# First batch of a Linformer attention and gated feed-forward kernel: fewer filler matmuls, head groups ordered by load landing, fewer visits in the second half

## The chip, the cores and the metric

The kernel runs on one core of a Trainium2 chip. The metric is the device time of one execution in microseconds. The profile's span (first to last instruction) is some 1.8 us shorter than the timed execution of the same run. In the profile's lines, PE is TensorE, DVE is VectorE, ACT is ScalarE and POOL is GpSimd, which issues most loads here. Each line gives start and length in us; brackets give the engine's idle time before it and what ended that wait.

## The reference, cut to what matters

```python
# q, k, v: (8 batches, 8 heads, 1024, 64); E, F: (64, 1024)
k_proj = np.einsum('ks,bhsd->bhkd', E, k)
v_proj = np.einsum('ks,bhsd->bhkd', F, v)
scores = scale * np.matmul(q, k_proj.transpose(0, 1, 3, 2))
attn = np.exp(scores - max); attn = attn / (sum + 1e-09)
x = np.matmul(attn, v_proj)      # then (8192, 512)
out = (sigmoid(x @ w_gate) * (x @ w_val)) @ w_out   # 512 -> 1536 -> 512
```

The attention of a batch is small; the feed-forward part (2304 matmuls of 512 columns) is what TensorE does for most of the time. In batches 1 to 7 the attention of the next batch is slipped between the feed-forward steps of the present one. Batch 0 has nothing to hide behind, so its first half (its "opening") is done before any feed-forward step can start.

## The kernel before

Parts that the change and the argument touch. A filler is a matmul whose result nobody reads:

```python
def busy(n):
    for _ in range(n):
        mm(FB[3], bank[FB[3]][:, 0:P], ident[:, :], ident[:, :], ["ident"])
```

The opening works on two groups R of four heads. `project` multiplies K or V by E or F, `qt` transposes Q, `sc` makes scores and exponentials, `den` their sums and reciprocals (VectorE: a reciprocal, a cast of it to bf16 and a step called the split, at L599, L605 and L610), `bc` spreads the reciprocals over partitions (ScalarE copies them out), `xo` multiplies by V and scales (VectorE):

```python
busy(20)
qt, sc, den, bc, xo = half_unit(0, whole)
for R in range(2):
    bk = whole.next()
    project(0, 0, [bk, bk], 0, R)
    busy(4)
    keep_k(bk, 0, R)
    turn_k(whole, R)
    busy(10 if R == 0 else 4)
...
qt(0, ("DVE", "ACT")); busy(6); sc(0)
qt(1, ("DVE", "DVE")); busy(6); sc(1)
den(0); busy(10); den(1); bc(0)
v_part(0)()            # V's first half: copies by ACT, DVE, ACT, DVE
busy(6); bc(1); xo(0); busy(4)
keep = v_part(1); keep()
```

The list of feed-forward steps of batch 0 starts with a pair of steps (four PSUM banks) and takes attention work at numbered slots: batch 0's second half at slots 5 to 10, batch 1's attention from 13 on:

```python
put(5, lambda: (qt2(0, ("DVE", "ACT")), qt2(1, ("DVE", "ACT"))))
put(6, lambda: sc2(0))
put(7, lambda: (den2(0), sc2(1)))
put(8, lambda: (den2(1), bc2(0)))
put(9, lambda: (xo2(0), bc2(1)))
put(10, lambda: xo2(1))
spots = (13, 14, 16, 16, 17, 18, 18, 21, 23, 24, 25)
# k_alone, turn_k, v_alone, sc(0), sc(1), den, split, bc(0), bc(1), xo(0), xo(1)
```

The softmax here doesn't subtract the row's maximum and nothing guards it: scores larger than these inputs give would overflow.

## Time and profile before

| | before |
|---|---|
| timed, median of 4 | 575.24 us (573.6 to 575.25) |
| span of the profiled run | 573.4 us |
| TensorE busy | 552.7 us, 96% |
| step after the first pair starts | 29.04 us |
| K of batch 1 is projected from | 57.05 us |
| V of batch 1 is projected from | 63.78 us |
| first output projection starts | 80.74 us |

The last four rows are starts of TensorE instructions in the timeline, counted from the span's start. They cut the head of the kernel in stages: the **opening** up to 29.04, the **second half** of batch 0 from there to 57.05 (28.01 us), and **batch 1's steps** from 63.78 to 80.74 (16.96 us). The lines that the prediction shows below are from this kernel.

### The profile page before, as it was taken

Reading aid. Unit: us, or ns where it says so; the run is one execution under the profiler, and the core shown is the slowest. Engines: PE = TensorE matmul, PEld = TensorE weight load, DVE = VectorE, ACT = ScalarE, POOL = GpSimd, SP = SyncE. Lnnn points to the kernel's source line nnn. Section 1 sums busy time; section 2 is a strip of 40 time slices with the busy share of each in tenths; the row PEclk is TensorE's granted clock in tenths of the full one; section 3 lists DMA queues with packets and bytes.
Section 4 is the critical chain, followed back from the end, with each engine's and each line's share of the span. In section 5 each row is a group of like instructions: output and inputs, shape, how many; then the busy total and the mean of one; then the engine's idle time right before and its main releaser. Section 6 shows DMA issues by size and latency. Waiting matters only on the chain.

```text
span 573.4 us, 7674 instructions
## 1 busy us (share of the span) xinstructions
PE 552.7 (96%) x2987; PEld 247.8 (43%) x3042; DVE 252.0 (44%) x403; ACT 176.5 (31%) x310; POOL 107.2 (19%) x148
## 2 busy tenths in 40 slices
PE   5799989999999999999999999999999999999997
PEld 5443434444444444444444444444444444444443
DVE  3546256325633546335452264434463354633332
ACT  2444641342224322333223422144223332222220
POOL 9400200104400071001800045000610007000000
PEclk9999999999999999999999999999999999999999
DMA  9999995964656169430696036660501101010012
GB/s 167 198 201 199 139 213 133 160 125 107 115 113 102 37 113 155 83 84 22 125 168 118 20 87 107 139 104 37 113 18 47 38 20 39 37 38 22 34 37 93
DMA packets 76421, 56.02 MB, mean 98 GB/s; under 512 B 34688, under 2 KB 67968, under 8 KB 76384
## 3 DMA queue, kind: packets, MB, share of 16 engines
q0 software_dynamic: 33984, 29.89, 34.5%
q1 hardware_dynamic: 42400, 25.63, 17.3%
q8 instruction: 24, 0.39, 0.3%
q14 instruction: 13, 0.11, 0.1%
HBM read 60.29 MB, written 16.78 MB: 134 GB/s over the span
## 4 chain that ended last, share of the span: by engine, by line
PE 95%; DVE 2%; issue 1%; DMA 1%; ACT 0%; SPq 0%; DVEq 0%
PE pF L227 87%; PE pA L227 7%; DMA EF<-in_F_dram 1%; DVE rden L786 1%; DVE xT L655 0%; DVE hT L941 0%; DVE rden L599 0%; ACT vpD L231 0%; DVE rhi L605 0%; DVE vpD L502 0%; DVE rhl L610 0%; DVE ost L968 0%; ACT qT L231 0%; SPq L314 0%; DVE rhi L795 0%
## 5 line engine op out<-in xcount | busy, mean ns | idle before, releaser
L941 DVE SCALAR_TENSOR_TENSOR hT<-sig,pF 128x512 bf16<-128x512 f32 x192 | 130.7, 685 | 202.3 <-PE pF L227 153.9
L231 ACT ACTIVATE sig<-pF 128x512 f32<-128x512 f32 x192 | 114.3, 599 | 318.3 <-PE pF L227 315.9
L227 PE MATMUL pF<-xT,wV 128*128 128x512 bf16 x751 | 195.9, 379 | 3.3 <-DVE hT L941 1.6
L227 PE MATMUL pF<-xT,wG 128*128 128x512 bf16 x748 | 194.8, 380 | 3.4 <-DVE xT L655 1.8
L227 PE MATMUL pF<-wO,hT 128*128 128x512 bf16 x750 | 173.9, 379 | 1.5 <-issue 0.8
L227 PEld LDWEIGHTS pF<-xT,wV 128*128 128x128 bf16 x768 | 75.1, 98 | 92.2 <-DVE hT L941 2.0
L227 PEld LDWEIGHTS pF<-wO,hT 128*128 128x128 bf16 x768 | 74.0, 98 | 93.0 <-issue 6.0
L227 PEld LDWEIGHTS pF<-xT,wG 128*128 128x128 bf16 x768 | 72.1, 98 | 97.2 <-issue 13.9
L832 POOL PARTITION_BROADCAST rb<-rrow x96 | 70.7, 798 | 217.1 <-DMA rrow<-rden 212.0
L968 DVE TENSOR_SCALAR ost<-pF 128x512 f32<-128x512 f32 x64 | 44.3, 692 | 103.0 <-PE pF L227 103.0
L857 DVE TENSOR_TENSOR xT<-pA,rb 128x512 bf16<-128x512 f32 x56 | 34.7, 681 | 0.0
L231 ACT ACTIVATE eT<-pA 128x512 bf16<-128x512 f32 x61 | 31.7, 602 | 8.9 <-PE pA L227 8.7
L786 DVE RECIPROCAL rden<-pA 128x128 f32<-128x128 f32 x28 | 23.7, 910 | 0.0
L245 POOL DMA_DIRECT2D KV<-in_v_dram x9 | 7.8, 875 | 84.9 <-PE pF L227 84.9
L227 PE MATMUL pA<-KV,EFT 128*64 128x512 bf16 (+2 forms) x168 | 16.0, 333 | 0.0
L245 POOL DMA_DIRECT2D KV<-in_k_dram x9 | 8.0, 890 | 36.8 <-PE pF L227 36.8
L231 ACT ACTIVATE kpd<-pA 64x1024 bf16<-64x1024 f32 x6 | 6.1, 1017 | 28.3 <-PE pA L227 28.3
L227 PE MATMUL pA<-qT,kpD 64*64 64x512 bf16 (+1 forms) x132 | 10.6, 373 | 1.2 <-ACT vpD L231 1.2
L227 PEld LDWEIGHTS pA<-KV,EFT 128*64 128x64 bf16 x168 | 8.3, 115 | 7.5 <-issue 3.6
L227 PE MATMUL pA<-eT,vpD 64*64 64x512 bf16 (+1 forms) x144 | 10.4, 364 | 0.2 <-DVE vpD L502 0.2
L231 ACT ACTIVATE vpD<-pA 64x512 bf16<-64x512 f32 (+2 forms) x20 | 9.7, 485 | 2.1 <-PE pA L227 1.7
L231 ACT ACTIVATE rb<-pA 128x512 f32<-128x512 f32 x14 | 7.4, 599 | 8.1 <-PE pA L227 8.1
(61 smaller groups left out, 97.5 us busy)
## 6 DMA issues: line engine op xcount, KB each, us to landing
out_dram<-ost SPq DMA_DIRECT2D x64, 256.0 KB, 2.1
Qb<-in_q_dram POOLq DMA_DIRECT2D x7, 1024.0 KB, 15.2
KV<-in_k_dram POOLq DMA_DIRECT2D x7, 1024.0 KB, 10.8
KV<-in_v_dram POOLq DMA_DIRECT2D x7, 1024.0 KB, 10.4
wO<-in_moe_w_out_dram POOLq DMA_DIRECT2D x1, 1536.0 KB, 12.2
wG<-in_moe_w_gate_dram POOLq DMA_DIRECT2D x5, 256.0 KB, 18.4
wV<-in_moe_w_val_dram POOLq DMA_DIRECT2D x5, 256.0 KB, 19.0
KV<-in_k_dram POOLq DMA_DIRECT2D x2, 512.0 KB, 7.8
```

The costliest lines, as they stand in the source:

```text
L227: return add("PE", lambda e: e.matmul(o, lhsT, rhs, **kw), r=r, x=[("bank", b)])
L231: return add("ACT", lambda e: e.activation(o, i, func, scale=scale), r=r, w=w, x=x)
L245: add("POOL", lambda e: e.dma_start(o, i), r=r, w=w, dma=sem)
L786: lambda e, cc=cc: e.reciprocal(rden[:, cc], bank[bk][:, cc]),
L832: lambda e, n=n, i=2 * rnd + c, j=j, parts=parts: e.partition_broadcast(rb[0:parts, n, :], rrow[32 * j : 32 * j + 1, i, :], channels=parts),
L857: lambda e, r=r, g=g, n=n, bk=bks[g]: e.tensor_tensor(xT[s][:, r, :, 256 * g : 256 * g + 256], bank[bk][:, :].rearrange("p (f c) -> p f c" ...
L941: lambda e: e.scalar_tensor_tensor(hT[blk % 2][:, m, :], sg[:, :], 1.0, bank[pv][:, :], ALU.add, ALU.mult,),
L968: lambda e: e.tensor_scalar(o[:, :], bank[pb][:, :], 0.5, None, op0=ALU.mult),
```

## The change

Its intent: take out matmuls that only keep the array busy, do each group's steps in the order in which the loads land, take V's first copies off VectorE (which carries the reciprocals), and serve the second half in fewer, larger visits that start one step sooner.

```diff
-        busy(20)
+        busy(6)
...
-            busy(4)
+            busy(3)
...
-            busy(10 if R == 0 else 4)
+            if R == 0:
+                busy(6)
...
         qt(0, ("DVE", "ACT"))
-        busy(6)
+        busy(3)
         sc(0)
         qt(1, ("DVE", "DVE"))
         busy(6)
+        den(0)
         sc(1)
-        den(0)
-        busy(10)
+        busy(4)
+        v_part(0, ["ACT"] * 4)
         den(1)
         bc(0)
-        v_part(0)()
-        busy(6)
-        bc(1)
+        busy(4)
         xo(0)
         busy(4)
-        keep = v_part(1)
-        keep()
+        bc(1)
+        busy(6)
+        v_part(1, ["ACT", "DVE", "ACT", "DVE"])
...
-                if blk == 0:
+                if blk <= 1:
                     ms = [[0, 1]] + ms[2:]
...
-                put(5, lambda: (qt2(0, ("DVE", "ACT")), qt2(1, ("DVE", "ACT"))))
-                put(6, lambda: sc2(0))
-                put(7, lambda: (den2(0), sc2(1)))
-                put(8, lambda: (den2(1), bc2(0)))
-                put(9, lambda: (xo2(0), bc2(1)))
-                put(10, lambda: xo2(1))
-                spots = (13, 14, 16, 16, 17, 18, 18, 21, 23, 24, 25)
+                put(4, lambda: (qt2(0, ("DVE", "ACT")), qt2(1, ("DVE", "ACT"))))
+                put(5, lambda: (sc2(0), sc2(1)))
+                put(6, den2)
+                put(8, lambda: (bc2(0), bc2(1)))
+                put(9, lambda: (xo2(0), xo2(1)))
+                spots = (12, 13, 15, 16, 17, 18, 18, 21, 22, 23, 24)
```

Cut: the new order of the PSUM banks in the opening, `den` for both groups at once, the order of the matmuls inside the first pair (all of a pair's first two input tiles, then the other two), and the slots of batch 2's loads and Q transposes, which move with the others. Since block 1 now starts with a pair too, its list has one slot less, and slot numbers from 12 on mean one step later than before. Old slot 16, used twice, stood for both V's projection and the first scores of batch 1; now they are at 15 and 16.

More of the change, by code (lines that the diff above doesn't have):

```diff
@@ L202, in bass_linformer_attn__then__ffn_glu_sigmoid_kernel @@
         whole = Ring(
-            (A0, A1)
-            + (A2, A3, F0, F1)
-            + (A0, A1)
-            + (F2, A2)
-            + (A3, A3)
-            + (F0, F1)
-            + (A0, A1)
-            + (A2, A0)
-            + (A3, F0)
-            + (F1, F2)
-            + (A1, A2)
-            + (A3, A0)
-            + (A1, A2)
+            (A0, A1, A2, A3, F0, F1)
+            + (A0, A1, F2, A2)
+            + (A3, F0, F1)
+            + (A0, A1, A3, F0)
+            + (A2, F2, A0, A1, F1)
+            + (A2, A3, A0, A1, A2, A3)
         )
@@ L582, in sc, with den @@
                     )
-            def den(R):
-                bk, pp = ring.next(), slice(64 * R, 64 * R + 64)
-                for n in (2 * R, 2 * R + 1):
+            def den(R=None):
+                bk = ring.next()
+                pp = slice(0, P) if R is None else slice(64 * R, 64 * R + 64)
+                for n in [2 * x + g for x in both(R) for g in range(2)]:
                     for c in range(4):
@@ L597, in den @@
                         )
-                dve(
-                    lambda e: e.reciprocal(rden[pp, 0:P], bank[bk][pp, 0:P]),
-                    [],
-                    [("rden", 0, R)],
-                    b=bk,
-                )
-                dve(
-                    lambda e: e.tensor_copy(rhi[pp, 0:P], rden[pp, 0:P]),
-                    [("rden", 0, R)],
-                    [("rhi", R)],
-                )
+                rd, ri, rl = ([k + (x,) for x in both(R)] for k in (("rden", 0), ("rhi",), ("rhl",)))
+                dve(lambda e: e.reciprocal(rden[pp, 0:P], bank[bk][pp, 0:P]), [], rd, b=bk)
+                dve(lambda e: e.tensor_copy(rhi[pp, 0:P], rden[pp, 0:P]), rd, ri)
                 dve(
                     lambda e: e.scalar_tensor_tensor(
-                        rhl[pp, 0:P], rhi[pp, 0:P], rows[pp, 3, 0:1], rden[pp, 0:P],
-                        ALU.mult, ALU.add,
-                    ),
-                    [("rden", 0, R), ("rhi", R), "rows"],
-                    [("rhl", R)],
+                        rhl[pp, 0:P],
+                        rhi[pp, 0:P],
+                        rows[pp, 3, 0:1],
+                        rden[pp, 0:P],
+                        ALU.mult,
+                        ALU.add,
+                    ),
+                    rd + ri + ["rows"],
+                    rl,
                 )
@@ L906, in mstep, with first_pair @@
             gate(blk, m, pbs["G"], pbs["V"])
-        def first_pair(between):
+        def first_pair(blk, between):
             pbs = {(m, n): ffn.next() for m in range(2) for n in "GV"}
-            for m in range(2):
-                for i in range(2):
+            for i in (0, 1), (2, 3):
+                for m in range(2):
                     for n in "GV":
-                        mm_one(0, m, i, n, pbs[m, n])
-                if m == 0:
-                    between()
-            for m in range(2):
-                for n in "GV":
-                    for i in (2, 3):
-                        mm_one(0, m, i, n, pbs[m, n])
-                gate(0, m, pbs[m, "G"], pbs[m, "V"])
+                        for ii in i:
+                            mm_one(blk, m, ii, n, pbs[m, n])
+                        if between:
+                            between()
+                            between = None
+                    if i == (2, 3):
+                        gate(blk, m, pbs[m, "G"], pbs[m, "V"])
         def mm_one(blk, m, i, n, pb):
@@ L989, in bass_linformer_attn__then__ffn_glu_sigmoid_kernel, with v_part @@
             project(0, 0, [bk, bk], 0, R)
-            busy(4)
+            busy(3)
             keep_k(bk, 0, R)
             turn_k(whole, R)
-            busy(10 if R == 0 else 4)
-        def v_part(R):
+            if R == 0:
+                busy(6)
+        def v_part(R, engines):
             bks = [whole.next(), whole.next()]
             project(1, 1, bks, 0, R)
-            return lambda: keep_v(bks, 0, ["ACT", "DVE", "ACT", "DVE"], R)
+            keep_v(bks, 0, engines, R)
         qt(0, ("DVE", "ACT"))
-        busy(6)
+        busy(3)
         sc(0)
@@ L1047, in bass_linformer_attn__then__ffn_glu_sigmoid_kernel @@
                     if len(m) == 2:
-                        todo.append(lambda: first_pair(lambda: xo(1)))
+                        todo.append(
+                            lambda blk=blk: first_pair(blk, None if blk else lambda: xo(1))
+                        )
                     else:
@@ L1078, in bass_linformer_attn__then__ffn_glu_sigmoid_kernel @@
             if b == 0:
-                put(17, lambda: load_next(2))
-                put(25, lambda: transpose_q(2))
+                put(16, lambda: load_next(2))
+                put(24, lambda: transpose_q(2))
             else:
```

## The prediction

> **What bounds the kernel now.** I read the page's first two parts first, then busy time by stage, then the chain of waits from start to end, and last the timeline of the stretches where that chain leaves TensorE. The page:
>
> ```profile
> PE 552.7 (96%) x2987; PEld 247.8 (43%) x3042; DVE 252.0 (44%) x403; ACT 176.5 (31%) x310; POOL 107.2 (19%) x148
> ...
> PE   5799989999999999999999999999999999999997
> ```
>
> TensorE is busy 96% of 573.4 us, and only the first slices (14.3 us each) show room. Busy time in four stretches: the opening up to the point where the first pair of feed-forward steps runs on without a stop, the rest of batch 0's attention, batch 1's attention beside it, and all the rest:
>
> ```profile
> 0.00:27.31 27.31, 17.92 (x241) 13.02 (x243) 13.94 (x49) 9.69 (x20) 19.75 (x33) 1.00 1.19 182
> 27.31:55.24 27.93, 26.60 (x181) 12.08 (x186) 14.95 (x25) 13.39 (x24) 0.00 (x0) 1.00 1.31 196
> 55.24:82.00 26.76, 23.84 (x151) 10.38 (x154) 11.49 (x17) 14.34 (x28) 3.65 (x4) 1.00 1.07 174
> 82.00:570.00 488.00, 484.36 (x2416) 212.32 (x2461) 210.90 (x312) 139.07 (x238) 83.82 (x111) 1.00 0.41 83
> ```
>
> The second column is the length, the third TensorE's busy time. TensorE idles 9.4, 1.3 and 2.9 us in the first three, and 3.6 us in the 488 us that the change does not touch. So the change can win some microseconds at the head, and nothing near 2% (11.5 us). Pieces of the chain of waits in the opening (start, length, what):
>
> ```profile
> 1.38 4.28 DMA EF<-in_F_dram
> 5.74 1.95 PE pA L227 x8
> 7.69 2.13 PE pF L227 x20
> ...
> 18.06 0.96 DVE rden L599
> 19.05 0.64 DVE rhi L605
> 19.71 0.34 DVE rhl L610
> 20.09 0.97 DVE rden L599
> ...
> 21.93 0.30 DVE vpD L502
> 22.37 0.41 PE pA L227 x8
> ...
> 26.49 0.69 DVE xT L655
> ```
>
> Twenty matmuls that compute nothing sit on the chain at 7.69; then two rounds of reciprocal, cast and split on VectorE follow one another, and V's copies come behind them. Later the chain leaves TensorE here (timeline; idle before it in brackets):
>
> ```profile
> 52.20 0.60 PE L227 MATMUL pF<-xT,wG 128*128 128x512 bf16 x2 [1.17 <-DVE xT L655]
> 66.55 0.41 PE L227 MATMUL pA<-qT,kpD 64*64 64x512 bf16 x3 [1.16 <-ACT vpD L231]
> 77.71 1.04 PE L227 MATMUL pF<-xT,wV 128*128 128x512 bf16 x4 [1.55 <-DVE hT L941]
> ```
>
> **When the loads land** decides what reordering can reach. The DMA view asked issue by issue gives the time from issue to landing; added to the issue's start: K's two halves at 1.34+7.0=8.3 and 2.23+8.7=10.9; Q's first two pieces at 12.3 and 13.5; V's halves at 4.44+11.6=16.0 and 5.17+14.5=19.7; the first gate and value weights at 20.3, 21.1, 21.8, 22.5, the second chunk at 23.8 and 25.1, the fourth at 31.7 and 33.1.
>
> **What the Trainium skill says.** "TensorE: Matmul & The Clock Gate", Part 1 (the HAM clock gate): the array runs at half rate until it has been busy for about 3.4 us, 107 ns against 56 ns per 128-column matmul. The trace agrees: 20 fillers from 7.48 took 2.34 us, (2.34-0.22)/19=112 ns apart; ten from 11.64 took 0.73, 57 ns apart. So fillers have a purpose, and removing them may leave the array cold longer. "SBUF — State Buffer", SBUF: two separate sides: VectorE and GpSimd have one port pair in common, locked by one for a whole instruction. The trace fits it without proving it: the same 64x128 cast took 0.63 us at 19.05, while POOL still issued loads, and 0.22 at 21.08, after its last. No other page bears on the order of steps.
>
> **Part 1, the opening.** The instruction order shows fillers going from 74 to 45: 20 become 6 before K, and so on. Step by step, with the durations of the kernel before:
> - The f32 transposes end at 7.69; six fillers at 112 ns end near 8.2. K's first half lands at 8.34 instead of being consumed at 9.75: projection 8.4 to 9.5 (1.06 at the cold clock). Its second half waits for its landing, 10.9, and the projection ends at 11.7 warm or 12.1 cold (before: 12.9). That is 1.3 us won; the rest of the 14 fillers' 1.55 us is lost to the load.
> - Q lands at 12.3: its transposes run at 12.4 instead of 13.89, ScalarE's copy ends near 13.65 (before 15.14), the second score group follows, and both exponentials are done at 15.2 (before 16.7).
> - Q's second group lands at 13.5 and now has two different banks, so the 0.5 us wait on the VectorE copy goes. The denominator of group 0 now comes before the scores of group 1: 15.2 to 15.5; its reciprocal starts at 15.6 against 18.06, 2.5 us earlier. Reciprocal 0.95, cast 0.63 (POOL is still issuing), split 0.34, with gaps: 17.5.
> - Scores of group 1 at 15.5 to 16.0; exponentials to 17.2. V's first half (landed 16.0) is projected 16.2 to 16.85, and ScalarE's four copies (0.28 each, 1.1 us) run 17.2 to 18.3. The second reciprocal runs 17.6 to 18.55, its cast and split to 19.6 (the cast now falls under POOL's issues as well, 0.4 us worse).
> - Broadcast of group 0 at 17.6; ScalarE copies it 18.3 to 19.4. The output product needs V at 18.3: 18.4 to 18.8. VectorE's two products run 19.6 to 20.95, behind the split. Before: 22.92 to 24.21.
> - V's second half lands at 19.7 and its bank is released by the first of those products at 20.3: projected 20.35 to 21.0, copied by 21.65. First gate matmuls 21.1; output product of group 1 at 21.7 to 22.1; two VectorE products, 1.29, to 23.4. The last eight matmuls of the pair run 23.5 to 25.2, and the value weights needed by then have landed at 22.5.
>
> Before, that last point is 29.04. So the opening gains 3.8 us by this sum. I take 3.3, because each hand-over I rounded can slip and none can jump ahead of a landing. The next weights (wG 23.8, wV 25.1) are just there, and the fourth chunk (31.7, 33.1) is needed at about 33: close, but met.
>
> **Part 2, batch 0's second half.** From the end of the Q transposes (38.56) to the end of the next block's first pair (55.24) the kernel before takes 16.7 us for seven feed-forward steps of 1.733 (12.1), so 4.6 beside them. After, eight steps (13.9) are in that stretch. Three attention visits of sixteen matmuls cost 0.7 each, 2.1, and some 0.1 of switching each. Merging batches ScalarE and VectorE work: four broadcast copies (2.1 us) delay the gate's activation, then four products (2.6) stand in front of the last step's product, so the pair waits some 0.3 us for its first operand and 0.65 for its fourth bank. That makes 4.2: a gain of 0.35. The 1.17 wait is thus mostly replaced, not removed. The single denominator saves VectorE 1.5 us that it does not need there.
>
> **Part 3, batch 1.** The list is one slot shorter, since the second block starts with a pair too. V's projection and the first scores, which shared a slot, are now one step apart: the 1.16 wait goes. In return the exponentials queue behind a gate activation (0.6 us at the denominators), and the 1.55 wait behind the four reciprocals becomes some 0.3 longer. Net 0.25. The output weights land at 58.95+12.2=71.2 and will be wanted at about 75 instead of 79: no wait. The remaining six batches do not change.
>
> **Sum:** 3.3+0.35+0.25=3.9, rounded to 4.0 us (0.7%): 575.2-4.0=571.2.
>
> **Rivals.** (a) The array stays cold: with fewer fillers the busy window that released the clock near 11.4 has holes of 0.3 to 0.5 us in 3.4. For it: before, the first window was also part empty and didn't release it. Against: six fillers stand in each wait. If it fails, some 3.4 us of small matmuls run at half rate, mostly under load waits: 1 to 1.5 us lost, 572.5. (b) Loads take the place of fillers: V's second half at 19.7 and the weights at 20.3 to 25.1 are fixed by a saturated DMA, so quicker steps only wait. That is in my sum for K, and V's half is only 0.7 us short of binding; if loads came 1 us later, 572. (c) Batched visits turn into a VectorE or ScalarE backlog worth more than I counted, 1 to 2 us: 572 to 573. (d) All hand-overs hold and the merged visits remove the waits whole: 5.5 us, 569.7.
>
> **Range and chances.** The three runs of before differ by 1.65 us on their own, and (a) and (c) together cost 2.5; (d) is the other end. So 569.3 to 573.3. Faster by over 2% would need 11.5 us, more than all idle time in the first stretch: 0.01. Slower by 2%: 0.005. Same: 0.985.
>
> **What would show it.** Right: K's first projection at 8.4; ten fillers' spacing near 57 ns by 12; first reciprocal near 15.6; the step after the first pair starting near 25.2; a wait before the second pair of about 1 us instead of 1.17; no wait on V's copies near 62; the stretch from 82 us on merely shifted by 4. Wrong: 112 ns spacing after 12 us, a wait on a weight or V load of over 0.5 us, VectorE's casts at 0.22, or a gain of the opening that later stretches give back.

## The result

| | before | after |
|---|---|---|
| timed, median of 4 | 575.24 us | 571.31 us (571.04 to 572.35) |
| ratio | | 0.9942 (95%: 0.992 to 0.9964) |
| span of the profiled run | 573.4 us | 569.3 us |
| step after the first pair | 29.04 | 27.43 |
| stage "second half" | 28.01 | 26.94 |
| stage "batch 1's steps" | 16.96 | 15.56 |

A ratio here is the mean time of one kernel's runs over that of the other's in the same rounds, so it is not quite the ratio of the medians. The time is 0.1 us from the predicted 571.2. The stages tell another story, though: predicted gains were 3.3, 0.35 and 0.25 us; the traces show 29.04-27.43=1.61, 28.01-26.94=1.07 and 16.96-15.56=1.40. The sum came out right and each of its three terms wrong.

The page after (first two parts):

```profile
PE 550.9 (97%) x2958; PEld 245.8 (43%) x3013; DVE 249.3 (44%) x398; ACT 177.0 (31%) x312; POOL 107.4 (19%) x148
...
PE   4999989999999999999999999999999999999997
```

29 matmuls fewer (2987 to 2958), which are the 29 fillers (74 to 45), and TensorE busy for only 1.8 us less: the rest of the 4.1 us of span is idle time gone. The busy time by stretch after; columns are the stretch, its length, then busy time of PE, PEld, DVE, ACT and POOL, clock, DMA share and GB/s. The limits are those of the prediction's table moved to the same events, except that the third ends at the start of the second output projection, some 1.8 us later in the work than the prediction's:

```profile
0.00:25.71 25.71, 16.91 (x212) 11.40 (x214) 12.94 (x47) 10.22 (x22) 19.78 (x33) 1.00 1.18 178
25.71:52.55 26.84, 26.08 (x181) 12.02 (x185) 12.98 (x22) 12.94 (x24) 0.00 (x0) 1.00 1.33 201
52.55:79.75 27.20, 25.33 (x162) 10.97 (x165) 12.44 (x19) 14.76 (x29) 3.66 (x4) 1.00 1.08 163
```

The first stretch is 1.6 us shorter (27.31 to 25.71), but its idle time is still 8.8 us where it was 9.4: much of the removed filler time turned into waiting. (Idle in the second stretch fell from 1.3 to 0.8 us, in the third from 2.9 to 1.9.) The timeline shows what was waited for at the start:

```profile
7.37 0.85 PE L220 MATMUL pF<-ident 128*128 128x128 bf16 x6
10.09 1.07 PE L220 MATMUL pA<-KV,EFT 128*64 128x128 bf16 x16 [1.88 <-DMA KV<-in_k_dram]
...
11.91 0.82 PE L220 MATMUL pF<-ident 128*128 128x128 bf16 x6
12.70 1.06 PE L220 MATMUL pF<-KV,EFT 128*64 128x128 bf16 x16
```

The six fillers end at 8.2 and TensorE waits 1.88 us for K's first half. In this run K landed 8.7 us after its issue at 1.34, at 10.05; in the trace of before it was 7.0, at 8.34. The six fillers at 11.91 are 0.12 us apart ((0.82-0.22)/5), so the array is still at half rate, where the kernel before had 57 ns at 11.64. Later waits of TensorE after, to set beside the three of before that the prediction shows:

```profile
48.59 0.60 PE L220 MATMUL pF<-xT,wG 128*128 128x512 bf16 x2 [0.18 <-DVE xT L645]
...
50.38 0.60 PE L220 MATMUL pF<-xT,wV 128*128 128x512 bf16 x2 [0.32 <-DVE hT L930]
...
75.37 1.04 PE L220 MATMUL pF<-xT,wV 128*128 128x512 bf16 x4 [1.55 <-DVE hT L930]
```

The first scores of batch 1 now start without a wait:

```profile
63.93 0.63 PE L220 MATMUL pA<-qT,kpD 64*64 64x512 bf16 x8
```

The 1.17 us wait has become two short ones, the 1.16 us wait on V's copies is gone, and the 1.55 us wait behind the reciprocals is what it was. From the first output projection to the end the span is 573.4-80.74=492.66 before and 569.3-76.66=492.64 after: nothing is given back later.

### The profile page after: what moved, and what is told of

Its sections match the earlier page's. It is cut to its first block, busy times and chain, and to the rows that moved or that the text cites. A ratio compares the mean times of both kernels' runs of the same rounds, so it can differ in the third digit from the quotient of the medians.

```text
span 569.3 us, 7617 instructions
## 1 busy us (share of the span) xinstructions
PE 550.9 (97%) x2958; PEld 245.8 (43%) x3013; DVE 249.3 (44%) x398; ACT 177.0 (31%) x312; POOL 107.4 (19%) x148
## 4 chain that ended last, share of the span: by engine, by line
PE 94%; DVE 2%; DMA 2%; issue 1%; ACT 1%; POOL 0%; DVEq 0%; POOLq 0%
PE pF L220 86%; PE pA L220 7%; DMA KV<-in_k_dram 2%; ACT eT L224 1%; DVE rden L776 1%; DVE hT L930 0%; DVE xT L645 0%; ACT sig L224 0%; DVE rden L593 0%; DVE ost L957 0%; ACT qT L224 0%; DVE vpD L495 0%; DVE rhi L785 0%; POOL quad L313 0%; DVE rhl L596 0%
## 5 line engine op out<-in xcount | busy, mean ns | idle before, releaser
L220 PE MATMUL pA<-eT,vpD 64*64 64x512 bf16 (+1 forms) x140 | 10.4, 366 | 0.3 <-DVE vpD L495 0.3
L220 PE MATMUL pA<-qT,kpD 64*64 64x512 bf16 (+1 forms) x140 | 10.4, 367 | 0.0
L238 POOL DMA_DIRECT2D Qb<-in_q_dram x11 | 9.4, 863 | 0.0
## 6 DMA issues: line engine op xcount, KB each, us to landing
KV<-in_v_dram POOLq DMA_DIRECT2D x7, 1024.0 KB, 11.7
```

The lines of the kernel that those rows point to most:

```text
L220: return add("PE", lambda e: e.matmul(o, lhsT, rhs, **kw), r=r, x=[("bank", b)])
L238: add("POOL", lambda e: e.dma_start(o, i), r=r, w=w, dma=sem)
```

## The experiments

Twelve runs were made after the result (three of them of unedited kernels), all with correct results. Since all have the same loads at the start, each trace is also a sample of when those loads land. Readings of all fourteen traces ("K landed": issue plus time to landing of K's first half; "full rate": start of the first group of fillers about 57 to 60 ns apart; the last three columns are the stages as above):

| trace | K landed | full rate by | step after first pair | second half | batch 1's steps |
|---|---|---|---|---|---|
| before | 8.3 | 11.6 | 29.04 | 28.01 | 16.96 |
| before_2 | 9.5 | 10.1 | 29.05 | 28.01 | 16.95 |
| before_3 | 9.5 | 10.4 | 29.03 | 28.02 | 16.96 |
| tail_only | 8.1 | 10.1 | 28.31 | 26.93 | 15.56 |
| after | 10.05 | 14.9 | 27.43 | 26.94 | 15.56 |
| rep_after | 9.5 | 14.4 | 27.04 | 26.94 | 15.56 |
| open_only | 9.4 | 18.6 | 28.06 | 28.02 | 16.96 |
| fill20 | 9.6 | 10.2 | 27.03 | 26.95 | 15.56 |
| k_first | 8.6 | 10.8 | 26.39 | 26.93 | 15.56 |
| v_alt | 9.5 | 14.4 | 27.55 | 26.93 | 15.55 |
| same_slot | 8.3 | 9.3 | 25.30 | 26.94 | 16.95 |
| visits6 | 9.8 | 16.7 | 27.77 | 26.67 | 15.56 |
| best1 | 9.4 | 10.1 | 27.03 | 26.67 | 15.56 |
| best2 | 9.1 | 11.3 | 26.17 | 26.67 | 14.58 |

The last two columns repeat to 0.02 us among kernels with the same steps. The third does not: it moves with the two columns before it, but not in step with them. Three traces stand at 29.03 to 29.05 and three at 27.03 or 27.04; fill20 and before_2 below show why.

**rep_after**: the changed kernel once more, no edit.

> The changed kernel once more, to see how much of its opening is chance. In the first trace of it K's first half landed at 10.05 us after the span's start, against 8.34 in the trace of the kernel before, and the array ran at 112 ns per filler until about 14. Theory 1 (landing is chance, about 1.7 us of spread): this trace shows another landing, 8.3 to 10.1, and with an early one the step after the first pair starts near 25.7 and the span is near 567.6. Theory 2 (the changed order itself delays the load): it lands near 10 again and the span is 569.3 again. Time in either case 569.5 to 572, ratio to before 0.992 to 0.995.

It took 570.71 us median of six (568.96 to 571.88), ratio 0.9918 (0.9901 to 0.9934). K landed at 9.5, the step after the pair started at 27.04. Two of the six executions were near 568.97, 1.74 us below the next three. Landing near 10 again fitted both theories, so this run decided nothing about the cause.

**open_only** and **tail_only** split the change in two.

```diff
# open_only: the changed opening; second half and batch 1 as before
-                put(4, ...) to put(9, ...); spots = (12, 13, 15, 16, ...)
+                put(5, ...) to put(10, ...); spots = (13, 14, 16, 16, ...)
-                if blk <= 1:
+                if blk == 0:
# tail_only: the opening (fillers, order, banks, first pair) as before; the rest changed
-        busy(6) ...
+        busy(20) ...
```

> Only the opening is changed (fillers, order, banks, V's copies); the second half of batch 0 and batch 1's steps are as before. Theory of the prediction (opening worth 3.3 of 3.9): 571.7 to 572.0, 3.3 us faster than before. Rival, from the two traces (opening 1.6, the rest 2.5): 573.6. Step after the first pair at 27.4 if K lands at 10, at 25.7 if at 8.3.

> The opening is as before; the second half of batch 0 in fewer visits and batch 1's moved steps as in the change. Theory of the prediction: only 0.6 us faster than before, 574.6. Rival, from the two traces (1.08 for the second half and 1.40 for batch 1): 2.5 us faster, 572.7. If the two parts add, this gain and that of the opening alone sum to the 4 us of the whole.

open_only: 573.64 us median, ratio 0.9968 (0.995 to 0.9986). tail_only: 572.4 us, ratio 0.9953 (0.9941 to 0.9966). Against a mean of before of 575.01 in these rounds, the means gain 1.78 and 2.63 us, 4.4 together; the whole change in the same rounds gained 4.69. The parts add within that spread. In both runs the rival reading fitted and the prediction's did not: open_only's interval (0.8 to 2.9 us) leaves out 3.3, and tail_only's (2.0 to 3.4) leaves out 0.6. That the later part is the larger one is clear from the stages of the traces (2.48 us), not from the times, whose intervals overlap. In its trace, open_only's array stayed at half rate until after 17 (its six fillers at 17.03 are 0.126 apart), and its step after the pair is the latest of the changed openings, 28.06; rep_after, with K landing at nearly the same time and full rate by 14.4, has 27.04. So being at half rate longer comes with about 1 us here.

**fill20**: the changed kernel with the first filler group back to twenty.

```diff
-        busy(6)
+        busy(20)
         qt, sc, den, bc, xo = half_unit(0, whole)
```

> The changed kernel with the twenty fillers of before ahead of K's projection instead of six (the other fillers stay as changed). Theory A (fewer fillers gain, since K lands at 8.3): 1.3 us slower than the changed kernel when K lands early. Theory B (K lands near 10, so that the removed fillers only turned into a wait, and the array leaves its half rate later without them): same as the changed kernel or up to 1 us faster, with the fillers' spacing at 57 ns by about 12 us instead of 14.5.

570.04 us median, ratio 0.9907; rep_after in the same rounds 570.71. The difference lies inside the spread of both. So with K landing late (9.6 here) taking out those fourteen fillers gained nothing, as theory B had it; theory A spoke of an early landing, which this trace does not have. The timeline shows why:

```profile
7.55 2.01 PE L220 MATMUL pF<-ident 128*128 128x128 bf16 x20
9.64 0.64 PE L220 MATMUL pA<-KV,EFT 128*64 128x128 bf16 x16
...
12.24 0.64 PE L220 MATMUL pF<-KV,EFT 128*64 128x128 bf16 x16 [0.73 <-DMA KV<-in_k_dram]
```

The twenty fillers end where K lands anyway, and the projections run in 0.64 us instead of 1.06. What the first projection wins is waited off at K's second half (12.24 against 12.25 in rep_after). What the second wins is kept for a while: both reciprocals start some 0.35 us sooner than in rep_after (16.88 and 18.88 against 17.22 and 19.23). It is lost only at the second cast. Here is that cast, after POOL's last load issue, in rep_after and then in fill20:

```profile
19.50 1.02 POOL L238 DMA_DIRECT2D KV<-in_v_dram  x1
20.23 0.35 DVE L594 CAST rhi<-rden 64x128 bf16<-64x128 f32 x1
```

```profile
19.48 1.03 POOL L238 DMA_DIRECT2D KV<-in_v_dram  x1
19.88 0.68 DVE L594 CAST rhi<-rden 64x128 bf16<-64x128 f32 x1
```

The casts start 0.35 us apart and end at 20.58 and 20.56, just after the issue (more under before_2). The step after the pair came at 27.03, against 27.04 of rep_after.

**k_first**: fill20, with POOL's four small memsets issued after K's loads.

```diff
-            for i in range(4): pool(... memset(quad ...))
             for R in range(2):
                 load_kv_heads(0, k, R)
+            for i in range(4): pool(... memset(quad ...))
```

> The run with twenty fillers ahead of K, and now the four memsets of the row numbers are issued by POOL after K's two loads instead of before them, so that K's loads are issued about 0.56 us sooner (1.34 to 0.78). Theory (K's landing ends the chain of the changed opening): K's halves land 0.5 us sooner, and the kernel is 0.3 to 0.6 us faster than that run, near 569.5. Rival (landing is set by the transfers of E and F or by chance in the queue): no change, 570.0, and the landing stays at 9.5 to 10.

570.01 us, ratio 0.9912, where fill20 had 0.9907: no gain shown. K's first issue moved from 1.34 only to 1.23, not to 0.78, with 0.80 us of idle before it that the record puts down to POOL's own queue; why the memsets could start at 0.73 and a load could not is open. The edit did not make the condition that it was to test, so the theory behind it stays untested; that K landed at 8.6 in this trace is inside the spread of the unedited kernels. The trace is still of use as one with twenty fillers and an early landing: K is projected only from 10.15, behind the fillers, where same_slot below, with six fillers and K at 8.3, projects from 8.59. The second projection starts 1.09 us later (12.06 against 10.97), and so does the step after the pair (26.39 against 25.30). This fits theory A of fill20, in one trace of each kernel.

**v_alt**: V's first half copied by ScalarE and VectorE in turn.

```diff
-        v_part(0, ["ACT"] * 4)
+        v_part(0, ["ACT", "DVE", "ACT", "DVE"])
```

> The changed kernel, but V's first half is copied by ScalarE and VectorE in turn as before, instead of by ScalarE alone. Theory of the change (VectorE carries the reciprocal chain, so ScalarE should take the copies): two VectorE copies of 0.29 push the second reciprocal, its split and the products back by up to 0.6 us: 0.3 to 0.6 slower than the changed kernel, 571.5. Rival (ScalarE's four copies of 1.1 us delay the broadcast copies as much): same, 571.0.

571.25 us, ratio 0.9934; the changed kernel had 0.9942 and 0.9918, so the time alone says nothing. The trace does: against rep_after, with K landing at 9.5 and full rate by 14.4 in both, the step after the pair is 0.51 us later (27.55 against 27.04). VectorE's lines, in v_alt and then the same reciprocal in rep_after:

```profile
19.21 0.62 DVE L495 CAST vpD<-pF 64x128 bf16<-64x128 f32 x2
19.86 0.96 DVE L593 RECIPROCAL rden<-pA 64x128 f32<-64x128 f32 x1
```

```profile
19.23 0.96 DVE L593 RECIPROCAL rden<-pA 64x128 f32<-64x128 f32 x1
```

The two copies of V stand ahead of the second reciprocal, which starts at 19.86 instead of 19.23. In this pair of traces the change's choice of ScalarE is worth that half microsecond, as its intent says.

**same_slot**: V's projection and the first scores of batch 1 in one slot again.

```diff
-                spots = (12, 13, 15, 16, 17, ...)
+                spots = (12, 13, 15, 15, 17, ...)
```

> The changed kernel, with V's projection and the first scores of batch 1 in one slot again as before. Reading of the two traces (batch 1 gained 1.4 us by their separation alone): the wait of 1.16 us on V's copies comes back and the kernel is 1.4 us slower than the changed one, 572.5. Term of the prediction (net 0.25 only, because the exponentials queue and the wait behind the reciprocals grow): 0.25 slower, 571.3.

572.12 us median, ratio 0.9942 (0.9923 to 0.9961), nearer to the first expectation; but one call of the changed kernel had the same ratio, so the trace has to decide. In it the wait is back:

```profile
61.74 0.41 PE L220 MATMUL pA<-qT,kpD 64*64 64x512 bf16 x3 [1.16 <-ACT vpD L224]
```

and the stage is 16.95 us, as before the change, against 15.56 with one step between the two. So the whole 1.40 us of batch 1 comes from this one slot. By chance the same trace is the one in which K landed early (8.3) and the array was at full rate by 9.3, and its opening is the one that the prediction had worked out:

```profile
10.97 0.64 PE L220 MATMUL pF<-KV,EFT 128*64 128x128 bf16 x16 [0.40 <-DMA KV<-in_k_dram]
...
15.61 0.95 DVE L593 RECIPROCAL rden<-pF 64x128 f32<-64x128 f32 x1 [0.55 <-PE pF L220]
16.59 0.58 DVE L594 CAST rhi<-rden 64x128 bf16<-64x128 f32 x1
...
17.61 0.96 DVE L593 RECIPROCAL rden<-pA 64x128 f32<-64x128 f32 x1
```

The prediction has these reciprocals at 15.6 and 17.6, and the step after the pair at 25.2; here it is 25.30. That execution took 570.35 us in spite of the wait put back; the other three took 572.11 to 572.45.

**visits6**: the second half in the six visits of before, but starting one step sooner as in the change.

```diff
-                put(5, lambda: (sc2(0), sc2(1)))
-                put(6, den2)
-                put(8, lambda: (bc2(0), bc2(1)))
-                put(9, lambda: (xo2(0), xo2(1)))
+                put(5, lambda: sc2(0))
+                put(6, lambda: (den2(0), sc2(1)))
+                put(7, lambda: (den2(1), bc2(0)))
+                put(8, lambda: (xo2(0), bc2(1)))
+                put(9, lambda: xo2(1))
```

> The changed kernel, with batch 0's second half in the six smaller visits of before, but starting one step earlier as in the change, so that a whole feed-forward step stands between the last output product and the block that reads it. Theory 1 (the gain of 1.08 us comes from the earlier start, and batching costs): the waits of 0.33 and 0.48 us before the pair go, one or two switches of 0.1 us come back, and it is 0.4 to 0.7 us faster than the changed kernel, 570.5. Theory 2 (the gain comes from fewer visits): 0.5 to 1 us slower, 571.8.

570.74 us, ratio 0.9923: between the two calls of the changed kernel, so no difference in time is shown. The stage in the trace is 26.67 us, 0.27 shorter than with batched visits, and no wait stands before the pair any more:

```profile
48.31 1.03 PE L220 MATMUL pF<-xT,wV 128*128 128x512 bf16 x4
49.17 0.60 PE L220 MATMUL pF<-xT,wG 128*128 128x512 bf16 x2
49.60 0.59 PE L220 MATMUL pF<-xT,wV 128*128 128x512 bf16 x2
```

best1 has the same 26.67. So fewer visits are not the source of the gain: they cost 0.27 of it. It comes from what visits6 keeps of the change, the start one step sooner and the pair at the head of block 1; no run separates these two.

**before_2** and **before_3**: the kernel before, unedited, to sample its loads.

> The kernel before, unchanged, for a second trace of its loads. In ten traces so far K's first half landed at 8.1 to 8.3 us in the two with the old opening and at 9.4 to 10.1 in all but one or two of those with the new one. Theory 1 (chance): this trace can land anywhere from 8.1 to 10.1, and with a late one the step after the first pair still starts near 29.0, since the old order reads K's second half only at 12.3. Theory 2 (the new order delays the loads): 8.1 to 8.4 again.

> The kernel before, a third trace, with the same two theories: 8.1 to 10.1 by chance, or 8.1 to 8.4 if the old opening lands early by its nature. Step after the first pair at 28.3 to 29.3.

575.22 and 575.18 us (one run each, state unknown). K landed at 9.5 in both, so the old opening does not land early by its nature: theory 1. And with K landing 1.2 us later than in the first trace, the step after the pair started at 29.05 and 29.03 instead of 29.04. The twenty fillers hide part of that (K is projected from 9.75, 9.55 and 9.59 in the three), and a cast on VectorE erases the rest. Rows of VectorE and POOL in before_2:

```profile
18.89 0.79 DVE L605 CAST rhi<-rden 64x128 bf16<-64x128 f32 x1
19.71 0.34 DVE L610 SCALAR_TENSOR_TENSOR rhl<-rhi,rows,rden 64x128 bf16<-64x128 bf16 x1
```

```profile
18.60 1.03 POOL L245 DMA_DIRECT2D KV<-in_k_dram  x1
19.47 1.04 POOL L245 DMA_DIRECT2D KV<-in_v_dram  x1
```

In the three traces of before this cast starts at 19.05, 18.89 and 18.94 and ends at 19.68, 19.68 and 19.67, each time 0.05 us after the end of the load issue of POOL in which it began (19.63, 19.63 and 19.62). The differences upstream are erased there. The same holds in all traces: of the 28 such casts, fifteen took 0.30 to 0.81 us instead of 0.22, and each of them began 0.26 to 0.76 us after the start of an issue and ended 0.04 to 0.06 us after its end. This fits a cast held by the issue that POOL was in. No run moved POOL's issues on purpose, but in k_first they ran 0.1 us later, and the end of the held cast moved with them (18.08, where best2's, under the same issue, ended at 17.94).

The old opening does not hide every landing, though. In tail_only, with K at 8.1, the first reciprocal is 0.64 us sooner than in before_2, so that its cast falls in the issue before:

```profile
18.26 0.57 DVE L601 CAST rhi<-rden 64x128 bf16<-64x128 f32 x1
```

It ends at 18.83 instead of 19.68, and the step after the pair comes at 28.31, 0.73 us sooner than in before. The timed executions of before lie mostly near 575.2 or 574.5, which are 0.7 us apart too; that these are the two cases is a guess, since no trace of one near 574.5 was kept.

**best1** and **best2**: versions to beat both kernels.

```diff
# best1: fill20 and visits6 together
# best2: best1, and batch 1's four reciprocals in two pairs a step apart
-                    den,
-                    split,
+                    lambda: den((0, 1)),
+                    lambda: (recips((2, 3)), split()),
-                spots = (..., 17, 18, 18, 21, 22, 23, 24)
+                spots = (..., 17, 18, 19, 21, 22, 23, 24)
```

> A version to beat both: the changed kernel with twenty fillers ahead of K and with six visits that start one step earlier. If the two gains add: 0.5 us from the sooner full clock on average and 0.3 from the visits (waits of 0.33 and 0.48 gone, switches back), 570.0 against 570.8 of the changed kernel. If the fillers are worth nothing when K lands early: 570.5.

> The run before it, and the four reciprocals of batch 1 split in two pairs with a feed-forward step between them. The wait of 1.55 us behind the four reciprocals should shrink to about 0.9 (the second pair and the split, 1.7 + 0.43 + 0.75, then stand before a later step's product): 0.7 us faster than the run before it, 569.4. Rival: VectorE has the same work before the broadcast, so the wait only moves: same.

best1: 570.44 us, ratio 0.9913 (0.9901 to 0.9924). best2: 568.67 us, ratio 0.9903 (0.9881 to 0.9924), with five of six executions between 568.61 and 569.57 and one at 572.42 (granted clock 0.994). In best2's trace the 1.55 us wait is gone and a shorter one has come at the broadcast:

```profile
73.84 0.39 PE L220 MATMUL pA<-rhl,bsel 32*128 32x512 bf16 x4 [0.69 <-DVE rhl L793]
```

The stage is 14.58 us, 0.98 less than in best1. The median is 2.6 us below the changed kernel's first result and 6.5 below before; against best1 the intervals overlap, so only the 0.98 us in the trace is shown.

## Why the prediction was right or wrong

**The total, the range and the verdict held**: 571.31 against 571.2. The limits of the argument held as well: all of the gain is in the first 80 us, and the rest of the span is 492.6 us in both kernels. Of the prediction's own signs, the result's trace shows some of each kind. As forecast for right: no wait on V's copies, and a last stretch merely shifted. As forecast for wrong: half-rate spacing after 12 us (three fillers at 13.70 are 0.14 apart) and the two casts at 0.22 and 0.23 us.

**The opening, predicted 3.3, was mis-sized by its conditions.** The step that failed is "K's first half lands at 8.34 instead of being consumed at 9.75". It took the landing of a single trace for a fixed time. In fourteen traces it was 8.1 to 8.6 in four and 9.1 to 10.05 in ten. The changed kernel's own trace had it at 10.05, 1.7 us late, and the array at half rate besides; rivals (a) and (b) both happened in it. Against the early trace (same_slot) its K projection starts 1.50 us later (10.09 against 8.59), its first reciprocal 2.14 (17.75 against 15.61) and the step after the pair 2.13 us later: 1.5 us stand at the landing, and the rest comes in before the first reciprocal, where the half rate lasted. The chain of steps itself was right: in the trace with an early landing and an early full rate (same_slot) the two reciprocals stood at 15.61 and 17.61 and the step after the pair at 25.30, against 15.6, 17.6 and 25.2. That is 3.74 us before 29.04, for a sum of 3.8, and 3.0 us against the old opening in the trace with the most similar conditions (tail_only, 28.31). The usual gain is smaller: 1.61 in the result's trace, 1.78 us in the timed means of open_only.

**The fillers.** "That is 1.3 us won" came only where K landed early: in same_slot the second projection ends at 11.61, for a predicted 11.7. With K late, twenty put back made the kernel no slower. The Trainium skill's "TensorE: Matmul & The Clock Gate", Part 1, and the trace of before were read rightly for the rate, 112 against 57 ns. The time of release was not: the prediction put it "near 11.4" as in one trace, and it was 9 to 18 us in others.

**The cast.** "The cast now falls under POOL's issues as well, 0.4 us worse" holds for some runs only: this second cast took 0.68 us in fill20, 0.22 or 0.23 in after and same_slot. It depends on where the cast falls against POOL's issues. The prediction had added a fixed cost; the traces show a fixed end, up to which earlier gains are lost.

**The second half, predicted 0.35, was 1.07.** The sum of 4.2 us beside the eight steps was too large: it measured 3.46 (35.23 to 52.55 is 17.32, less eight times 1.733). The text also lists three visits of 0.7 where the kernel has four, so its listed terms add to some 3.35 and not to its 4.2, which needs a fourth visit of 0.8. The timeline puts the four at about 0.57, 0.59, 0.35 and 0.74 (the third corrected for one missing matmul record), 2.25 in all; the two waits were 0.33 and 0.48 by the starts of the rows, 0.81 against the 0.95 predicted; the 0.40 left over fits its 0.1 at each of the four switches. So what was too large is the size given to a visit (0.7 against 0.56 on average) and to the waits. "Mostly replaced, not removed" was right for the 1.17 us wait, and visits6 shows what the batching cost: 0.27 us.

**Batch 1, predicted 0.25, was 1.40.** That the separation removes the 1.16 us wait was right; same_slot brings it back to the hundredth. The two costs set against it failed: the denominators did not wait 0.6 us (their eight matmuls took 0.67 us against 0.62), and the wait behind the reciprocals did not grow by 0.3: 1.55 in both.

The errors, -1.7, +0.7 and +1.15 us, cancelled to 0.2 in the traces and 0.1 in the times. That is luck: a comparison of the time alone would have hidden it.

## What to carry to other kernels

A filler ahead of a load costs nothing if the load ends the wait anyway, so read the landing from several traces before counting its removal as a gain; the order of steps can only be as early as the latest usual landing. Put one long step between a producer that another engine must copy out and its consumer: that single slot was worth 1.40 us here, more than all merging of visits, which cost 0.27. Check a predicted sum stage by stage, since a right total can be three wrong terms. Where stages of different kernels end at the same hundredth although earlier steps differ by 0.3 us, look for a step whose end is set by something else, as the cast's was.

## What the Trainium skill lacked or had wrong

- "TensorE: Matmul & The Clock Gate", Part 1, gives a warm-up of about 3.4 us of activity. From a first matmul at 5.5 to 6.1 us, fillers were first seen at full rate between 9.3 (same_slot) and 18.6 us (open_only), in openings with waits of 0.2 to 1.9 us between short bursts. The page says that the moment varies, by 0.5 us for matmuls back to back, and that idle gaps matter; it gives no figure for a start that is only partly busy, where it was up to some 9 us apart between two traces.
- "SBUF — State Buffer", section SBUF: two separate sides, describes a VectorE operation that holds up a load issued by POOL. The traces here fit the reverse, which its exclusive lock allows but whose timing beside a load issue it does not give: fifteen of 28 casts of 64x128 took 0.30 to 0.81 us instead of 0.22, began 0.26 us or more after the start of a load issue of POOL and ended 0.04 to 0.06 us after its end. Four that began at most 0.12 us after an issue's start took 0.22 or 0.23, so the hold does not seem to begin with the issue. No run isolates it.
- No page that I read gives the spread of a load's landing from run to run. The same 512 KB load issued at 1.34 us landed 6.8 to 8.7 us later in thirteen traces.
